# Later raw weight units, an earlier second q group, idle matmuls in the first steps and three rotating buffers in a fused retention + Mish MLP + SwiGLU kernel

## The chip, the cores and the metric

The kernel runs on one core of one Trainium2 chip. The metric is the device time of one execution in microseconds (us). Before the change, three runs took 933.38, 936.87 and 937.66 us; the median is 936.87.

## The reference

Everything is float32. q, k and v have shape [4, 8, 576, 64] (batch, head, position, head dimension); x has 2304 rows of 512.

```
scores = q @ k.T / sqrt(64)
ret    = (scores * D) @ v            D[i, j] = gamma_h ** (i - j) for i >= j, else 0
x      = ret, heads joined           [2304, 512]
h      = x @ w_in                    [512, 2048]
x      = (h * tanh(softplus(h))) @ w_out          [2048, 512]
g, val = x @ w_gate, x @ w_val       [512, 1536] each
out    = (silu(g) * val) @ w2_out    [1536, 512]
```

## The kernel before, in words

All instructions are issued in an order written out by hand; every engine works its own list in that order. A float32 product is made of three products of rounded parts (high x high, high x low, low x high), so each weight and each activation is split into a high part (a cast on ScalarE) and a low part (a subtraction on VectorE or GpSimd).

**Retention** (`retention`, from L312) has 20 steps, 5 per batch: four of 128 positions, one of 64. A step `t` (loop at L585) runs `inter` (queries times the running state, L516), `scores` (L456, L445), `state` (second half of the chunk, L497), `transposes` of the next k (L409, copied to kT by ScalarE, L411), `q_ahead` with half 1, `masks` (VectorE, L470), `products` (masked scores times v, L529, and the scaling by `gout` on VectorE, L539), the first half of the next chunk's `state`, `q_ahead` with half 0, and `scale` of v two steps ahead (GpSimd, L426). `q_ahead` (L390) says which halves of which q group (two chunks each) are transposed in which step. SyncE loads k and v four steps ahead and q six (L336 to L357). `warm` (L572) issues idle matmuls of zeros; `W` says how many.

**Raw units.** The 32 units of w_in and w_out (512 KB each) are fetched raw (`fetch`, L94, into 4 buffers), re-scaled (`rebias_raw`, L104: ScalarE L106 and VectorE L107), given sign and low bits (`sign` L111, `join` L115), and split (`part`, L117). `conversions` (L127) is the list of these pieces; retention takes one per step from step 1, and another in the steps of `EARLY` (9, 11, 14, 17), in which a first-layer product `g1` also runs.

**The Mish MLP** runs in slots `s` = 4 to 63 (`slot`, L707): `g1` (first layer, L627), then second-layer matmuls of four slots earlier (L913, L670), `mish` (ScalarE, L687), `g_hi` (L696), `g_lo` (VectorE, L700). Slots below 32 alternate between token blocks 0 and 1 (384 tokens each); slots 32 to 47 are block 2, 48 to 63 block 3. Before a block begins, its x is split (`split_hi`, ScalarE L294; `split_lo`, VectorE L299): block 2 in slots 30 and 31, block 3 in slots 44, 45 and 47.

**Background work.** Each slot from 25 (`PREP`) on ends with pieces of two lists, paced by `Pace`: a piece is issued when the sum of the paces (`RATES`) reaches its cost. `third` makes Strassen combinations of w_in for the last two token blocks (`group1`). `second` (`pieces`, L241) converts the gate and value weights: 12 groups of two raw units (`group`, L169), each loaded (`raw_load`, L149), re-scaled, joined, combined and written back to DRAM (`put`, L154, through 4 small buffers `c`); behind the first four groups stands the conversion of one unit of w2_out (`last`). Groups up to 6 ask for the next pair when their own last write is issued, into the same two buffers.

**Strassen parts.** The last two blocks' first layer runs as Strassen products (`pair1`, 8 x 7 = 56 steps, L875 te, with second-layer matmuls L913 ea between); from its second 7 steps on, each step ends with a part of `second`, and from step 45 (`AHEAD`) VectorE and ScalarE also make the operands of the next part (`ysteps`, L821, L828, L832). Then the gate and value products follow (L875 t, L1051 fa).

## Time and profile before

| | before |
|---|---|
| median of 3 runs | 936.87 us (933.38 to 937.66) |
| profiled execution: own time, span | 936.48 us, 934.7 us |
| busy: TensorE, weight load | 907.2 us (97%), 847.4 us (91%) |
| busy: VectorE, ScalarE, GpSimd | 545.5 us, 378.6 us, 50.9 us |
| mean granted TensorE clock | 0.984 |
| chain that ended last | TensorE 84%, VectorE 6%, DMA 5%, ScalarE 3%, issue 2% |

PE is TensorE's matmuls, PEld its weight loads, DVE is VectorE, ACT ScalarE, POOL GpSimd; SPq and ACTq are the queues on which SyncE and ScalarE issue transfers. Times in the trace count from the start of the span. The granted clock is a share of 2.4 GHz; 0.50 is the level of 1.2 GHz.

### The profile page before, as it was taken

To read this page: it belongs to the slowest core of one execution; us is meant where nothing else is said; L and a number is where in the kernel's file an instruction comes from. 1 tells how busy PE (TensorE), PEld (TensorE's weight loads), DVE (VectorE), ACT (ScalarE), POOL (GpSimd) and SP (SyncE) were. 2 spreads that over 40 slices of the span, in tenths; PEclk is the share of its full clock that TensorE was granted. 3 is DMA by queue.
4 is the path that set the end of the run, shared out by engine and by line. 5 is a ranking of instruction groups with operands and counts; after the bars stand their busy time and mean duration, and the time that the engine had idled before them with its cause. 6 is when DMAs were issued, how large, how long until landed. Compare 5 with 4: busy or idle time off the path is not lost.

```text
span 934.7 us, 17118 instructions
## 1 busy us (share of the span) xinstructions
PE 907.2 (97%) x6788; PEld 847.4 (91%) x6788; DVE 545.5 (58%) x1090; ACT 378.6 (41%) x788; POOL 50.9 (5%) x55
## 2 busy tenths in 40 slices
PE   7899899999999799999999999999999999999998
PEld 7788799999899799989998999999999999999997
DVE  1343468767797686567764666666544556544444
ACT  2475556644654454445444333323222223222222
POOL 2253400000000000000000000000000000000000
PEclk7799999999999899999999999999999999999999
DMA  9967445554697666599866566644745544644421
GB/s 198 226 147 176 114 117 172 155 154 154 242 294 255 214 205 225 170 305 320 300 209 240 190 204 204 206 159 154 229 161 164 159 161 154 228 161 159 158 91 68
DMA packets 125648, 177.68 MB, mean 190 GB/s; under 512 B 47104, under 2 KB 84608, under 8 KB 125568
## 3 DMA queue, kind: packets, MB, share of 16 engines
q1 hardware_dynamic: 123904, 176.19, 59.9%
q8 instruction: 54, 0.88, 0.4%
q10 hardware_dynamic: 1664, 0.39, 0.2%
q14 instruction: 26, 0.21, 0.1%
HBM read 133.04 MB, written 43.52 MB: 189 GB/s over the span
## 4 chain that ended last, share of the span: by engine, by line
PE 84%; DVE 6%; DMA 5%; ACT 3%; issue 2%; SPq 0%; POOL 0%; DVEq 0%; ACTq 0%; POOLq 0%
PE t L875 27%; PE fa L1051 16%; PE h L627 10%; PE ea L913 6%; PE da L913 6%; PE te L875 6%; PE acc L670 3%; PE o L516 2%; PE state L497 2%; PE o L529 2%; DMA rawv<-in_moe_w_val_dram 1%; DMA rawg<-in_moe_w_gate_dram 1%; PE tk L409 1%; PE tq L378 1%; PE s L456 1%
## 5 line engine op out<-in xcount | busy, mean ns | idle before, releaser
L875 PE MATMUL t<-y,su 128*128 128x384 f32 x1512 | 306.5, 338 | 1.2 <-ACT p L1123 0.7
L875 PEld LDWEIGHTS t<-y,su 128*128 128x128 f32 x1512 | 270.8, 188 | 24.8 <-DVE cv L882 1.8
L1051 PE MATMUL fa<-fu,g 128*128 128x512 f32 x648 | 190.0, 395 | 0.1
L627 PE MATMUL h<-xs,u 128*128 128x384 f32 x672 | 129.6, 339 | 7.5 <-ACT xs L294 5.0
L627 PEld LDWEIGHTS h<-xs,u 128*128 128x128 f32 x672 | 117.0, 190 | 9.9 <-ACT xs L294 5.3
L1051 PEld LDWEIGHTS fa<-fu,g 128*128 128x128 f32 x648 | 118.5, 188 | 7.6 <-ACT g L1074 0.5
L1074 ACT CAST g<-sg 128x384 fp32r<-128x384 f32 x72 | 37.0, 513 | 173.8 <-DVE sg L1110 120.5
L913 PE MATMUL ea<-ge,u 128*128 128x512 f32 (+1 forms) x384 | 75.9, 336 | 0.0
L913 PE MATMUL da<-g,u 128*128 128x512 f32 (+1 forms) x384 | 71.7, 336 | 0.0
L875 PE MATMUL te<-ye,eu 128*128 128x384 f32 x336 | 67.9, 337 | 1.0 <-DVE ve L882 1.0
L913 PEld LDWEIGHTS ea<-ge,u 128*128 128x128 f32 x384 | 62.0, 188 | 5.7
L913 PEld LDWEIGHTS da<-g,u 128*128 128x128 f32 x384 | 60.4, 188 | 6.6
L1099 ACT ACTIVATE sg<-sg 128x384 f32<-128x384 f32 x54 | 28.4, 526 | 90.7 <-DVE sg L882 90.7
L1079 DVE TENSOR_TENSOR g<-sg,g 128x384 fp32r<-128x384 f32 x72 | 40.2, 558 | 40.6 <-ACT g L1074 40.6
L670 PE MATMUL acc<-g,u 128*128 128x384 f32 x336 | 62.7, 335 | 0.0
L700 DVE TENSOR_TENSOR g<-m,g 128x384 fp32r<-128x384 f32 x60 | 33.4, 557 | 45.7 <-ACT g L696 45.7
L875 PEld LDWEIGHTS te<-ye,eu 128*128 128x128 f32 x336 | 56.8, 188 | 3.2 <-DVE ve L882 1.3
L670 PEld LDWEIGHTS acc<-g,u 128*128 128x128 f32 x336 | 58.7, 188 | 0.0
L687 ACT ACTIVATE m<-h 128x384 f32<-128x384 f32 x64 | 31.3, 489 | 44.6 <-PE h L627 44.1
L882 DVE TENSOR_TENSOR u<-t,p 128x384 f32<-128x384 f32 x36 | 20.0, 556 | 44.0 <-PE t L875 40.6
L882 DVE TENSOR_TENSOR v<-t,p 128x384 f32<-128x384 f32 x36 | 20.0, 556 | 35.3 <-PE t L875 34.6
L696 ACT CAST g<-m 128x384 fp32r<-128x384 f32 x64 | 32.9, 514 | 1.8
(129 smaller groups left out, 1055.0 us busy)
## 6 DMA issues: line engine op xcount, KB each, us to landing
su<-comb SPq DMA_DIRECT2D x126, 512.0 KB, 3.3
comb<-c SPq DMA_DIRECT2D x84, 256.0 KB, 2.6
eu<-ecomb SPq DMA_DIRECT2D x28, 512.0 KB, 5.3
raw<-in_moe_w_in_dram SPq DMA_DIRECT2D x16, 512.0 KB, 4.0
raw<-in_moe_w_out_dram SPq DMA_DIRECT2D x16, 512.0 KB, 3.7
ecomb<-e_s SPq DMA_DIRECT2D x32, 256.0 KB, 2.3
rawg<-in_moe_w_gate_dram SPq DMA_DIRECT2D x12, 512.0 KB, 5.8
ecomb<-u SPq DMA_DIRECT2D x24, 256.0 KB, 4.7
```

The lines of the kernel that those rows point to most:

```text
L627: nc.tensor.matmul(ps, lhsT=u[:, a, kk * 128:(kk + 1) * 128], rhs=s[:, e, :], start=(c == 0), stop=(c == n - 1),)
L670: nc.tensor.matmul(accs[b][d][:, :T], lhsT=u[:, a, d * 128:(d + 1) * 128], rhs=g[:, e, :], start=(i == 0 and c == 0), stop=(i == F1 - 1 an ...
L687: nc.scalar.activation(w, hs.pop(s), AF.Mish)
L696: nc.scalar.copy(out=gs[s][:, 0, :], in_=ws[s])
L700: eng.tensor_tensor(out=g[:, 1, :], in0=ws.pop(s), in1=g[:, 0, :].bitcast(F32), op=ALU.subtract)
L875: nc.tensor.matmul(p, lhsT=w[:, a, kk * 128:(kk + 1) * 128], rhs=y[kk][:, x, :], start=begin and kk == 0 and (a, x) == (0, 0), stop=kk == ...
L882: nc.vector.tensor_tensor(out=out_, in0=a, in1=b_, op=ALU.add)
L913: nc.tensor.matmul(o, lhsT=u[:, a, d * 128:(d + 1) * 128], rhs=y[:, :512] if r == 0 else y[:, 512:], start=f == 0 and (a, x) == (0, 0) and ...
L1051: nc.tensor.matmul(accs["f", b][m], lhsT=gs[u, e, h][:, x, m * 128:(m + 1) * 128], rhs=fu[2 * (u % PAIRS) + e][:, a, :], start=first, stop ...
L1074: nc.scalar.copy(out=gs[u, e, h][:, 0, :], in_=x)
L1079: nc.vector.tensor_tensor(out=g[:, 1, :], in0=x, in1=g[:, 0, :].bitcast(F32), op=ALU.subtract)
L1099: nc.scalar.activation(x, bank_ if part_ is None else x, AF.Silu)
```

## The change

- `fetch` of raw units: in retention at steps 0, 2 and 4 (before: 0, 1, 2, 4), and from the third `first` piece on instead of the second; one more fetch after the loop.
- `gout` is loaded by SyncE behind k and v of step 1, not by ScalarE; q group 1 is loaded ahead of k of step 2.
- The first half of q group 1 is transposed at the end of step 0, the second early in step 1; `masks` is issued ahead of `transposes` and `q_ahead`.
- Idle matmuls: 10 instead of 3 ahead of the first `state`; 3 at the start of steps 0 and 1, 2 ahead of their `products`. They write another bank.
- Block 2's x is split whole in slot 30, in which no background piece runs; none in slot 31.
- `second`: paces 1.9, 1.2 and 1.1 instead of 2.1, 1.3 and 1.3; the first unit of a pair is re-scaled and joined ahead of the second; each unit is loaded on its own; the buffers of groups 5 to 7 rotate over three; the empty pieces behind groups go.

```diff
--- before.py
+++ after.py
@@ -47,10 +47,10 @@
     NA = 10
     RAW, XS = 4, 6
     OFF = 2
-    W = (12, 3, 3)
+    W = (12, 3, 10, 3, 3, 2)
     PREP = 25
     NC = 4
-    RATES, AHEAD = (2.1, 1.3, 1.3, 1.15, 3.3), 45
+    RATES, AHEAD = (1.9, 1.2, 1.1, 1.15, 3.3), 45
     EARLY = (9, 11, 14, 17)
 
     xp = ctx.enter_context(tc.tile_pool(name="xp", bufs=1))
@@ -131,6 +131,7 @@
                 sign(j)
                 if j:
                     part(j - 1, splits[0])
+                if j > 1:
                     fetch()
             yield 1.4, first
             if j + 1 < len(todo):
@@ -171,13 +172,12 @@
         keys = [f"{'gv'[z]}{i}_{e}" for e in range(2)]
         v = {}
 
-        def load():
-            for e in range(2):
-                raw_load(keys[e], cols((w2_gate, w2_val)[z], 2 * i + e), False, e + 2 * (n >= FREE and n % 2))
-                lo, hi = words(keys[e])
-                for h in range(2):
-                    v[f"a{e + 1}{h + 1}"] = lo[:, h * KH:(h + 1) * KH].bitcast(F32)
-                    v["s" + "1324"[2 * e + h]] = hi[:, h * KH:(h + 1) * KH].bitcast(F32)
+        def load(e):
+            raw_load(keys[e], cols((w2_gate, w2_val)[z], 2 * i + e), False, BUFFERS.get(n, ((0, 1), (2, 3))[n % 2 == 0])[e])
+            lo, hi = words(keys[e])
+            for h in range(2):
+                v[f"a{e + 1}{h + 1}"] = lo[:, h * KH:(h + 1) * KH].bitcast(F32)
+                v["s" + "1324"[2 * e + h]] = hi[:, h * KH:(h + 1) * KH].bitcast(F32)
 
         def puts(*names):
             for nm in names:
@@ -185,9 +185,8 @@
                 put(v[nm], comb[i][c // 2][:, c % 2], f"c{i}_{c}", nc.vector)
 
         return load, [
-            (0.55, lambda: rebias_raw(keys[0])), (0.55, lambda: rebias_raw(keys[1])),
-            (0.7, lambda: sign(keys[0])), (0.7, lambda: join(keys[0])),
-            (0.7, lambda: sign(keys[1])), (0.7, lambda: join(keys[1])),
+            (0.55, lambda: rebias_raw(keys[0])), (0.7, lambda: sign(keys[0])), (0.7, lambda: join(keys[0])),
+            (0.55, lambda: rebias_raw(keys[1])), (0.7, lambda: sign(keys[1])), (0.7, lambda: join(keys[1])),
             (0.85, lambda: puts("a11", "a12")), (0.85, lambda: combine(v, ("s1", "s3"))),
             (0.45, lambda: puts("a22")), (0.85, lambda: combine(v, ("s2", "s4"))),
             (0.85, lambda: puts("s1", "s3")), (0.85, lambda: puts("s2", "s4")),
@@ -224,7 +223,11 @@
             (0.85, lambda: combine(v, ("s2", "s4"))), (0.85, lambda: puts("s2", "s4")),
         ]
 
-    FIRST, FREE = 4, 7
+    FIRST, FREE = 4, 8
+    BUFFERS = {**{n: (0, 1) for n in range(FIRST + 1)}, 5: (2, 0), 6: (1, 2)}
+    BEGIN = {4: ((5, 0),), **{n: ((n + 1, 0), (n + 1, 1)) for n in range(FREE, 2 * PAIRS - 1)}}
+    END = {**{n: ((n + 1, 0), (n + 1, 1)) for n in range(FIRST)},
+           4: ((5, 1), (6, 0)), 5: ((6, 1), (7, 0)), 6: ((7, 1), (8, 0), (8, 1))}
 
     def last(i):
         key = f"f{i}"
@@ -240,21 +243,19 @@
 
     def pieces():
         gr = [group(n) for n in range(2 * PAIRS)]
-        gap = [(0.8, lambda: None)] * 2
+        yield 0.0, lambda: gr[0][0](0)
+        yield 0.0, lambda: gr[0][0](1)
+        yield from [(0.8, lambda: None)] * 2
         for n, (load, steps_) in enumerate(gr):
-            f_load, behind = last(n) if n < FIRST else (None, gap)
-            if n == 0:
-                yield 0.0, load
-                yield from gap
-            if n >= FREE and n + 1 < len(gr):
-                yield 0.0, gr[n + 1][0]
-                behind = []
-            yield from steps_[:2]
+            f_load, behind = last(n) if n < FIRST else (None, [])
+            for m, e in BEGIN.get(n, ()):
+                yield 0.0, lambda m=m, e=e: gr[m][0](e)
+            yield from steps_[:3]
             if f_load:
                 yield 0.0, f_load
-            yield from steps_[2:]
-            if n < FREE:
-                yield 0.0, gr[n + 1][0]
+            yield from steps_[3:]
+            for m, e in END.get(n, ()):
+                yield 0.0, lambda m=m, e=e: gr[m][0](e)
             yield from behind
 
     class Pace:
@@ -390,13 +391,13 @@
             def q_ahead(t, half):
                 b, sc, n = steps[t]
                 due = (
-                    ((b, 1, 1),) if b else (),
-                    ((b, 2, 0),) if b else ((b, 1, 1), (b, 1, 0)),
+                    ((b, 1, 1),) if b else ((b, 1, 0),),
+                    ((b, 2, 0),) if b else ((), (b, 1, 1)),
                     ((b + 1, 0, 0),) if b else ((b + 1, 0, 0), (b, 2, 0)),
                     ((b + 1, 0, 1),),
                     ((b + 1, 1, 0),),
                 )[sc]
-                if half < len(due):
+                if half < len(due) and due[half]:
                     q_transposes(*due[half])
 
             def transposes(t):
@@ -552,7 +553,6 @@
             for c in range(2):
                 nc.scalar.dma_start(out=mask[C * c:C * c + C], in_=mask_d[C * c:C * c + C, C * c:C * c + C])
             nc.scalar.dma_start(out=gv, in_=gv_d)
-            nc.scalar.dma_start(out=gout[:, :, :128], in_=gout_d)
             nc.scalar.dma_start(out=gstep, in_=gstep_d)
             for e in range(2):
                 nc.scalar.dma_start(
@@ -560,18 +560,19 @@
                 )
             load(1, "k", k)
             load(1, "v", v)
+            nc.sync.dma_start(out=gout[:, :, :128], in_=gout_d)
+            load_q(2)
             load(2, "k", k)
-            load_q(2)
             load(2, "v", v)
             load(3, "k", k)
             load(3, "v", v)
 
 
-            idle = ps1.tile([128, 2, 512], F32, tag="s", name="idle")
+            idle = pha.tile([128, T], F32, tag="h", name="idle")
 
             def warm(n):
                 for _ in range(n):
-                    nc.tensor.matmul(idle[:, 0, :128], lhsT=zero, rhs=zero, start=True, stop=True)
+                    nc.tensor.matmul(idle[:, :128], lhsT=zero, rhs=zero, start=True, stop=True)
 
             warm(W[0])
             q_transposes(0, 0, 0)
@@ -583,12 +584,15 @@
             state(0, 0)
             scale(1)
             for t in range(len(steps)):
+                if t < 2:
+                    warm(W[3 + t])
                 inter(t)
                 scores(t)
                 state(t, 1)
+                masks(t)
                 transposes(t + 1)
                 q_ahead(t, 1)
-                masks(t)
+                warm(W[5] if t < 2 else 0)
                 if t in EARLY:
                     g1(EARLY.index(t))
                     zeroth.one()
@@ -613,9 +617,10 @@
                     load_q(4)
                     load_q(5)
                 load_q(t + 6)
-                if t in (0, 1, 2, 4):
+                if t in (0, 2, 4):
                     fetch()
             splits[0] = nc.vector
+            fetch()
 
     with tc.manual_schedule():
         def prod(ps, u, nm, j):
@@ -712,10 +717,8 @@
             if not i and s >= 2 * F1:
                 g1(s)
             d, nm = xt, "x"
-            if s < 2 * F1 - 2:
-                parts = ()
-            elif s < 2 * F1:
-                parts = [(2, 2 * (s % 2) + k) for k in range(2)]
+            if s < 2 * F1:
+                parts = [(2, kk) for kk in range(KT)] if s == 2 * F1 - 2 else ()
             elif b + 1 == NC:
                 parts = ()
             else:
@@ -730,7 +733,7 @@
             if s >= 2 * F1 + LAG:
                 g2_out(s - LAG)
             zeroth(RATES[4])
-            if s >= PREP:
+            if s >= PREP and not (parts and s < 2 * F1):
                 third(RATES[3])
                 second(RATES[s >= NS - F1 + 3])
 
```

## Rows read from the trace of the kernel before

**Rows 1.** The page, busy time of each engine

```profile
PE 907.2 (97%) x6788; PEld 847.4 (91%) x6788; DVE 545.5 (58%) x1090; ACT 378.6 (41%) x788; POOL 50.9 (5%) x55
```

**Rows 2.** A 23.4 us stretch: busy per engine, granted clock, DMA share, GB/s

```profile
304.20:327.60 23.40, 17.18 (x88) 16.46 (x87) 15.13 (x35) 11.51 (x27) 1.19 (x2) 0.85 0.62 217
```

**Rows 3.** TensorE's waits over the span: us in total, times, longest

```profile
PE h L627 <- ACT xs L294: 5.0, 1, 5.0
PE o L529 <- DVE p L470: 2.8, 2, 2.2
PE h L627 <- DVE xs L299: 2.5, 2, 1.3
...
PE s L445 <- issue: 1.8, 1, 1.8
...
PE te L875 <- DVE ve L882: 1.0, 1, 1.0
PE o L516 <- DVE qT L380: 1.0, 1, 1.0
PE t L875 <- ACT p L1123: 0.7, 1, 0.7
```

**Rows 4.** SyncE's waits over the span

```profile
SPq L102 <- POOL u L122: 39.3, 7, 10.9
```

**Rows 5.** Timeline of TensorE in the first five steps

```profile
10.64 0.85 PE L497 MATMUL state<-vs,k 64*64 64x64 f32 x16 [2.29 <-POOL vs L426]
...
32.88 0.69 PE L529 MATMUL o<-p,vs 64*64 64x64 f32 x32
...
45.22 0.62 PE L516 MATMUL o<-qT,sbd 64*64 64x64 f32 x13
```

**Rows 6.** Two stretches of retention, columns as in rows 2

```profile
11.00:22.00 11.00, 10.54 (x216) 9.74 (x212) 1.45 (x3) 2.28 (x6) 5.13 (x5) 0.53 1.02 210
...
41.00:45.20 4.20, 4.18 (x50) 3.38 (x49) 1.45 (x3) 0.96 (x2) 1.70 (x2) 0.59 0.77 252
```

**Rows 7.** Timeline: three idle matmuls (two instructions each)

```profile
7.52 0.83 PE L574 MATMUL idle<-zero 128*128 128x128 f32 x6
```

**Rows 8.** Raw unit 0: its issue by SyncE, and that transfer's time to landing

```profile
19.42 2.19 SPq L102 DMA_DIRECT2D raw<-in_moe_w_in_dram  x1
...
DMA to landing us min/median/max: 6.5/6.5/6.5
```

**Rows 9.** Timeline: issue of gout on ScalarE's queue

```profile
3.15 0.60 ACTq L555 DMA_DIRECT2D gout<-const_dram  x1
```

**Rows 10.** The page, transfers by line: KB each, median us to landing

```profile
raw<-in_moe_w_in_dram SPq DMA_DIRECT2D x16, 512.0 KB, 4.0
```

**Rows 11.** Timeline at block 2's split

```profile
228.36 0.48 ACT L687 ACTIVATE m<-h 128x384 f32<-128x384 f32 x1
...
238.17 3.23 PE L627 MATMUL h<-xs,u 128*128 128x384 f32 x17 [1.32 <-DVE xs L299]
```

**Rows 12.** Timeline before block 3: a load, its second half's first piece

```profile
301.89 1.33 SPq L151 DMA_DIRECT2D rawg<-in_moe_w_gate_dram  x2
...
308.54 0.68 ACT L106 ACTIVATE rawg<-rawg 128x512 f32<-128x512 f32 x1 [0.74 <-DMA rawg<-in_moe_w_gate_dram]
```

**Rows 13.** Timeline of VectorE: the four kinds of background pieces

```profile
240.20 0.76 DVE L107 TENSOR_SCALAR rawv<-rawv 128x512 uint32<-128x512 uint32 x2
240.87 0.69 DVE L111 SCALAR_TENSOR_TENSOR rawv<-rawv 128x512 uint32<-128x512 uint32 x1
...
242.41 0.88 DVE L167 TENSOR_TENSOR e<-e 128x256 f32<-128x256 f32 x2
...
475.20 0.76 DVE L157 TENSOR_TENSOR c<-rawv,c 128x256 fp32r<-128x256 f32 x2
```

**Rows 14.** Strassen part one, its end; columns as in rows 2

```profile
479.00:497.00 18.00, 18.00 (x106) 16.84 (x105) 13.15 (x27) 8.05 (x18) 0.00 (x0) 1.00 0.49 166
```

**Rows 15.** Transfers by queue, 38 to 39 us: packets, MB, engine share

```profile
q1 hardware_dynamic: 750, 0.19, 114.5%
q8 instruction: 1, 0.02, 8.8%
```

## The prediction

> **What bounds the kernel now.** I read the page first: TensorE is busy for 907.2 of 934.7 us [rows 1]. So what can be won is 27 us of idle time and whatever runs at the low clock; work taken from another engine is worth only what TensorE waits for it. The table of stretches then shows that it lies in retention, and in one stretch in which TensorE was busy for 17.2 of 23.4 us at a granted clock of 0.85 [rows 2]. TensorE's waits name the causes [rows 3]: 5.0 us for the split of a token block on ScalarE and 2.5 us for its second half on VectorE (two waits, 1.3 and 1.2); 2.8 us for masked scores; 1.8 us of "issue"; 1.0 each for q transposes and for one Strassen sum. SyncE's own waits show one more thing: 39.3 us of standing behind a raw unit whose buffer GpSimd had not emptied, with the k, v and q loads queued behind it [rows 4]. That one costs TensorE nothing by itself in rows 3.
>
> The early steps are the other loss. The first state product starts at 10.6, after 2.3 us without work; step 2's last products start at 32.9, step 5 at 45.2 [rows 5]. From 11 to 22 TensorE was busy for 10.5 of 11 us, but the mean granted clock was 0.53; at 41 to 45, after the 1.8 us gap, it was 0.59 [rows 6]. So a gap of about 2 us before a stretch brings the 1.2 GHz level, and the loss of the second drop is 4.2 x (1 - 0.59) = 1.7 us.
>
> **Retention, part by part.** Three parts act together. (a) Idle matmuls: 7 more before the first state product, 10 more in steps 0 and 1. Three cost 0.83 us at the high level [rows 7], 0.28 each. The seven lie in the 2.3 us wait for v and cost nothing (7 x 0.28 = 2.0); the ten cost 2.8 us at most, and if the clock stays low up to twice that. (b) masks moved ahead of the transposes' copies, and q group 1 transposed in step 0 and early in step 1: this removes the 2.2 us of rows 3 (the longest of the 2.8) that masked scores waited behind a q copy, and the 1.0 for the q copy itself. (c) Loads: raw units 1 to 3 leave the start.
>
> What would be late next? From step 2's products to step 5 are 12.3 us, three steps of 4.1 [rows 5]. Were the high level held from 10.6, two and a half such steps and 2.8 us of idle matmuls would bring step 2's products near 24. But the piece that rescales raw unit 0 still stands at the end of step 1, on ScalarE and VectorE, and raw unit 0 is asked for at 19.4 and lands 6.5 us later, at 25.9 [rows 8]. Today the piece comes late enough not to wait. Sooner, it waits, and step 2's masks stand behind it on VectorE, the state copy and k copy on ScalarE. So step 2's products start at 25.9 + 0.4 (shift) + 0.7 (mask) = 27.0, against 32.9: 5.8 us sooner. Before them TensorE idles for some 3 us, and I charge one clock drop of 1.6 (3.2 us at the low level, as after the gap of rows 6). From there to step 5 I leave the 12.3 us of today (45.2 - 32.9), with its "issue" wait, since the transfers around it are the same. Term: 5.8 - 1.6 = **4.2 us**. Bounds: 2.4 us worse (low level throughout: the ten idle matmuls at twice 0.28, 5.6, for the 3.2 that (b) removes) and 9 us better (no drop, and the 1.8 with its 1.7 gone).
>
> The constant gout goes from ScalarE's queue, where its issue took 0.60 us, to SyncE's, ahead of q group 1, k2 and raw unit 0 [rows 9]; bytes and engines stay. I take nothing for it: it also frees v's first transfer from a competitor. The Trainium skill ("DMA: Bandwidth & Descriptors", Issuing engines are not separate DMA queues) says that transfers of all issuing engines interleave on the same 16 engines and that the choice saves only issue time. By that rule the move wins no bandwidth and puts 0.6 us ahead of raw unit 0: the term would be 3.6 and the total 0.6 higher. No run here shows it yet.
>
> Raw units 3 to 8 are then asked for one program piece before their first use instead of several. Their landing took 4.0 us in the median [rows 10]. I take nothing: SyncE no longer meets a buffer still in use there, so it reaches the request up to a step early. After retention the wait on the same buffer decides, and nothing moves.
>
> **Block 2's split** in one go at slot 30. Now ScalarE reaches that slot's activation at 228.4, and TensorE, wanting the last quarter at 236.9, waits until 238.2 [rows 11]. The activation, four casts, g's cast and its subtraction and four subtractions, estimated at 0.5 each, end by 228.4 + 11 x 0.5 = 233.9, and no piece of the background work runs in that slot. Term: **1.3 us**, bounds 0 and 1.3.
>
> **Block 3's split.** The chain of waits runs through the background conversion of the gate and value weights: the load of a new pair is issued at 301.9 only after the old pair is written out, its second half starts on ScalarE at 308.5 [rows 12], and the split queued behind it is 5.0 + 1.2 = 6.2 us late. Stretch 304 to 328 also lost 0.15 x 23.4 / 2 = 1.75 us to the clock [rows 2]. With the change, the paces give at slot 46: before 22 slots x 2.1 = 46.2 units, after 21 x 1.9 = 39.9, so 6.3 units less are behind it. A group of 8.6 units costs VectorE 7 subtractions at 0.38, 4 combinations at 0.44, 2 shifts at 0.38 and 4 sign or join steps at 0.69 [rows 13]: 7.9 us, 0.92 per unit. That is 5.8 us, and the load itself moves from slot 45 to slot 48, behind the split. Both together exceed 6.2 us. Full gain 7.9; I take **7.0**, since slot 46 now holds four writes whose small buffers can wait for their transfers. Bounds 3 and 7.9.
>
> **The Strassen wait of 1.0** [rows 3] came of a pair asked for two steps before use. Now half of it is loaded a group earlier and the other half three steps ahead. Term **1.0**, bounds 0 and 1.1. Removing the empty pieces costs nothing: TensorE's work covers them.
>
> **What the slower pace pushes back.** By the paces, the background work ends some ten steps later, in step 52 of the 56 of the first Strassen part, not 43. In steps 45 to 55 VectorE also makes the next part's operands: it was busy for 13.2 of 18.0 us there [rows 14]. One group and two subtractions more, 8.7 us, make 21.9: 3.9 us of backlog. Two products lie between a sum and the next use of its bank, which hides some of a backlog; at the part's end, where TensorE already waited 0.7 [rows 3], nothing does. I charge half: **2.0 us lost**, bounds 0 and 4.
>
> **Sum.** 4.2 + 1.3 + 7.0 + 1.0 - 2.0 = 11.5 us against the profiled execution's own 936.5 (span 934.7 and 1.8 around it). It lies 0.4 below the median of the runs, 936.9. I predict **925 us**. A measurement of this kernel can tell about 0.5%, 4.7 us, from no change.
>
> **Rivals.** (1) *The idle matmuls don't hold the clock* (chance 0.15): they only add work at the low level, and retention gives -2.4 instead of 4.2: 936.5 - (1.3 + 7 + 1 - 2 - 2.4) = 931.6. For it: 10.5 us of busy TensorE left the clock at 0.53 [rows 6]. Against: there a gap of 2.3 us had come just before [rows 5], which the seven now fill. (2) *Block 3's wait only moves* (0.10): another write or load stands ahead of slot 47's split, only 3 of its 7.9 us are won, and the backlog costs 4: 936.5 - (4.2 + 1.3 + 3 + 1 - 4) = 931. (3) *Fetches go free* (0.12): the "issue" wait at 41 follows a packet of the instruction queue at 38 to 39, among 750 packets of data [rows 15]: I take it for a fetch that came late. Fewer raw units in the start could remove it and its drop, 3.5 us, and block 3's and the backlog's terms come at their better ends: 936.5 - (7.7 + 1.3 + 7.9 + 1 - 0) = 919. The Trainium skill ("Runtime: NRT & Kernel Launch", Instruction fetch mechanics) holds the fetch to be mostly hidden; by it that wait has another cause, and the sum stays at 925. No row here separates the two. (4) *Slower* (0.05): the raw units 3 to 7, asked for one piece ahead in steps 8 to 17, stop ScalarE and VectorE as raw unit 0 does. If each lands only after 6.5 us [rows 8] and SyncE comes to it only in its own step of some 4 us, every one waits 2.5 and drops the clock once: 5 x (2.5 + 1.6) = 20.5, and 925 + 20.5 = 945.5. It decides where request to landing exceeds the distance to the next piece; at 4.0 [rows 10] it doesn't. (5) *The split is not sooner in effect*, because VectorE reaches slot 30 late: 1.3 us, within the range.
>
> **Numbers.** The forecast, with terms within a few us of mine, has 0.58. The range reaches from the better bounds of most terms (914) to rival 2 with a poor start (934); beyond it lie rival 4 and the ends of the rest, some 0.2. Faster by over 0.5% (below 932.2) is the forecast (0.56 of its 0.58), rival 3, and half of rivals 1 and 2: 0.80; within 0.5%: the rest, 0.15; slower: 0.05.
>
> **What would show it.** Right: no wait of TensorE for xs L299 near 237 or xs L294 near 305, and a clock of 1.00 in 304 to 328; step 2's products near 27 with VectorE or ScalarE waiting for raw unit 0; a clock above 0.9 from 11 to 22; some waits on te or t between 485 and 510. Wrong: a clock near 0.5 from 11 to 22, a new wait for a raw unit in steps 9 to 17, or a split still late at block 3.

## The result, and the profile after

Four runs of the changed kernel took 920.96, 921.2, 922.67 and 922.98 us, median 921.93; four of the kernel before on the same chip 933.38 to 937.66, median 936.35. The ratio is 0.9851 (95% interval 0.9823 to 0.9878): faster by 14 us, 1.5%, where 11.5 had been forecast. The profiled execution took 920.96 us, span 919.1, mean granted clock 0.994 (0.984 before).

The page's busy times and its row of the granted clock, which answer to [rows 1]:

```profile
PE 903.7 (98%) x6822; PEld 844.2 (92%) x6822; DVE 546.5 (59%) x1090; ACT 376.9 (41%) x788; POOL 50.6 (6%) x55
...
PEclk9799999999999999999999999999999999999999
```

TensorE's idle time fell from 27.5 to 15.4 us (span less busy), and only the second of the 40 slices, 23 to 46 us, still shows a low clock. TensorE's waits over the span, against [rows 3] (us in total, times, longest):

```profile
PE s L457 <- issue: 2.5, 2, 1.6
PE o L530 <- DVE p L471: 2.1, 1, 2.1
PE t L878 <- DVE scratch L885: 1.3, 2, 0.7
...
PE t L878 <- ACT p L1126: 1.0, 1, 1.0
PE state L498 <- issue: 0.9, 2, 0.6
```

The waits for xs (5.0 and 2.5) and the one for te (1.0) are gone; "issue" is now the largest, and t has waits at the end of Strassen part one. To see where the time came from, I compare the start of the same instruction in both timelines, one where each stage begins:

| first ... | before | after | won in the stage before it | forecast |
|---|---|---|---|---|
| products of step 2 | 32.9 | 27.0 | 5.9 | 5.8 |
| inter of step 5 | 45.2 | 40.7 | -1.4 | -1.6 |
| da (retention done) | 119.0 | 110.7 | 3.8 | 0 |
| acc behind block 2's split | 253.8 | 243.9 | 1.6 | 1.3 |
| te (Strassen part one) | 376.8 | 359.6 | 7.2 | 7.0 |
| fa (gate and value products) | 524.7 | 509.2 | -1.6 | -1.0 (1.0 less 2.0) |
| end | 934.7 | 919.1 | 0.1 | 0 |

Stretches of after (columns as in [rows 2]): the one of [rows 2], that of [rows 6] from 11 to 22, and four of 2 us at steps 2 to 4.

```profile
304.20:327.60 23.40, 22.73 (x130) 22.24 (x130) 18.78 (x43) 12.23 (x30) 1.21 (x2) 1.00 0.62 217
...
11.00:22.00 11.00, 10.42 (x287) 9.47 (x287) 4.28 (x8) 3.61 (x8) 5.44 (x6) 1.00 0.95 191
26.00:28.00 2.00, 0.79 (x34) 0.66 (x34) 1.15 (x3) 1.65 (x4) 0.00 (x0) 0.98 1.28 233
28.00:30.00 2.00, 1.87 (x18) 1.65 (x18) 1.17 (x3) 0.37 (x1) 0.00 (x0) 0.50 1.19 265
36.00:38.00 2.00, 2.00 (x29) 1.67 (x30) 0.78 (x3) 1.29 (x3) 0.00 (x0) 0.50 1.31 173
38.00:40.00 2.00, 1.97 (x48) 1.69 (x44) 0.59 (x2) 1.58 (x3) 0.93 (x1) 0.96 1.25 219
```

TensorE is busy for 22.7 of 23.4 us where it was busy for 17.2, at 1.00. The clock stands at 1.00 from 11 to 22 (0.53 before). In retention it falls once, behind a gap of 2.1 us, and stays at 0.50 from 28 to 38. What made that gap, in the timeline of after (start, us, instruction, in brackets the idle time before it and its releaser):

```profile
20.59 0.58 SPq L102 DMA_DIRECT2D raw<-in_moe_w_in_dram  x1
...
25.94 0.43 DVE L107 TENSOR_SCALAR raw<-raw 128x512 uint32<-128x512 uint32 x1 [4.10 <-DMA raw<-in_moe_w_in_dram]
25.94 0.70 ACT L106 ACTIVATE raw<-raw 128x512 f32<-128x512 f32 x1 [3.65 <-DMA raw<-in_moe_w_in_dram]
26.28 0.68 DVE L471 TENSOR_TENSOR p<-s,mask 128x512 f32<-128x512 f32 x1
...
27.02 0.69 PE L530 MATMUL o<-p,vs 64*64 64x64 f32 x32 [2.08 <-DVE p L471]
```

This is the predicted chain: raw unit 0 lands at 25.94, VectorE and ScalarE have stood for it for some 4 us, and behind it come mask and products, at 27.0.

One thing had not been foreseen: steps 5 to 19 won 3.8 us. TensorE's larger "issue" waits of after in the timeline, and the hardware queues in the microseconds that hold the instruction-queue packet ahead of each (44 to 45 and 50 to 51; packets, MB, share of the 16 engines):

```profile
46.83 0.46 PE L457 MATMUL s<-qT,kT 64*64 64x64 f32 x15 [0.93 <-issue]
52.62 0.58 PE L457 MATMUL s<-qT,kT 64*64 64x64 f32 x24 [1.61 <-issue]
```

```profile
q1 hardware_dynamic: 691, 0.19, 123.9%
q8 instruction: 1, 0.02, 8.6%
...
q1 hardware_dynamic: 937, 0.25, 108.9%
q8 instruction: 1, 0.02, 5.6%
```

Before, there were such waits at 41.0 (1.79), 82.5 (1.44) and 104.8 (1.46), some 3 us behind packets at 38 to 39, 79 to 80 and 102 to 103, with data shares of 114.5% [rows 15], 109.2% and 125.4%. The last two are rows of the waits of before that [rows 3] leaves out:

```profile
PE o L516 <- issue: 1.5, 1, 1.5
PE o L529 <- issue: 1.4, 1, 1.4
```

After has none later than 52.6, though twelve more packets come in retention, in microseconds with data shares of 0 to 101.4%.

### The profile page after: what moved, and what is told of

Its sections match the earlier page's. It is cut to its first block, busy times and chain, and to the rows that moved or that the text cites. A ratio compares the mean times of both kernels' runs of the same rounds, so it can differ in the third digit from the quotient of the medians.

```text
span 919.1 us, 17207 instructions
## 1 busy us (share of the span) xinstructions
PE 903.7 (98%) x6822; PEld 844.2 (92%) x6822; DVE 546.5 (59%) x1090; ACT 376.9 (41%) x788; POOL 50.6 (6%) x55
## 4 chain that ended last, share of the span: by engine, by line
PE 87%; DVE 4%; issue 2%; DMA 2%; ACT 2%; SPq 2%; POOL 1%; DVEq 0%; POOLq 0%; ACTq 0%
PE t L878 28%; PE fa L1054 16%; PE h L632 13%; PE da L916 7%; PE acc L675 6%; PE ea L916 6%; PE te L878 5%; PE o L517 1%; PE state L498 1%; PE o L530 1%; SPq L358 1%; PE acc L891 1%; DVE y L835 1%; PE tq L379 1%; PE tk L410 1%
## 5 line engine op out<-in xcount | busy, mean ns | idle before, releaser
L632 PE MATMUL h<-xs,u 128*128 128x384 f32 x672 | 127.2, 336 | 0.0
L632 PEld LDWEIGHTS h<-xs,u 128*128 128x128 f32 x672 | 115.6, 188 | 1.4
L885 DVE TENSOR_TENSOR u<-t,p 128x384 f32<-128x384 f32 x36 | 20.0, 556 | 44.0 <-PE t L878 40.7
L701 ACT CAST g<-m 128x384 fp32r<-128x384 f32 x64 | 32.9, 514 | 1.8
```

Source lines behind the costliest of these rows:

```text
L632: nc.tensor.matmul(ps, lhsT=u[:, a, kk * 128:(kk + 1) * 128], rhs=s[:, e, :], start=(c == 0), stop=(c == n - 1),)
L701: nc.scalar.copy(out=gs[s][:, 0, :], in_=ws[s])
L885: nc.vector.tensor_tensor(out=out_, in0=a, in1=b_, op=ALU.add)
```

## The experiments

The theory after the result: the idle matmuls hold the clock; raw unit 0's landing sets step 2; at block 3 the slower pace, with the loads moved, takes the background work out of the split's way; and steps 5 to 19 went faster because the moved raw units leave DMA room for TensorE's instruction blocks. The rivals: the idle matmuls do nothing; the loads, or the pace, alone free block 3; the raw units' place is worth nothing. Each kernel is the changed one with one edit; "first da" (110.7 in after) tells the end of retention. "before" stands for the kernel before on the same chip.

| run | median us (runs) | ratio to before, 95% | first da |
|---|---|---|---|
| after | 921.93 (4) | 0.9851, 0.9823 to 0.9878 | 110.7 |
| e1 | 926.55 (4) | 0.9922, 0.9892 to 0.9953 | 113.1 |
| e2 | 920.29 (4) | 0.9848, 0.9821 to 0.9875 | 108.6 |
| e3 | 921.4 (4) | 0.9856, 0.9828 to 0.9884 | 113.4 |
| e4 | 929.68 (10) | 0.9955, 0.9936 to 0.9974 | 109.7 |
| e5 | 920.98 (4) | 0.9855, 0.9831 to 0.9879 | 110.2 |
| e6 | 920.4 (4) | 0.9848, 0.9816 to 0.988 | 111.2 |
| e8 | 920.26 (4) | 0.9854, 0.9819 to 0.9889 | 110.3 |
| e9 | 921.33 (4) | 0.9864, 0.9832 to 0.9896 | 113.1 |
| e13 | 919.21 (5) | 0.9839, 0.9812 to 0.9867 | 110.7 |
| e10, e11, e12 (one run each) | 937.56, 925.78, 921.79 | | 117.8, 115.8, 110.3 |

Retention is the same code in after, e3, e4 and e6. Its end lies between 109.7 and 113.4 there, and the masks of step 5 start between 38.4 (e4) and 41.9 (after); a difference of under 4 us in such a time decides nothing by itself.

**e1: without the new idle matmuls.**

```diff
-    W = (12, 3, 10, 3, 3, 2)
+    W = (12, 3, 3, 0, 0, 0)
```

> The changed kernel with the idle matmuls as before the change: 3 ahead of the first state product, none in steps 0 to 2; everything else kept. Theory A (the idle matmuls hold TensorE's clock): the granted clock falls to 0.5 within steps 0 and 1, step 2's last products start 1 to 4 us after the 27.0 of the changed kernel, and the whole takes 925 to 928 us. Theory B (the earlier masks and q transposes do it alone): steps 0 and 1 run at 1.00 without them, or the wait for raw unit 0 (landed at 25.9) hides the difference: products at 27.0 again and 921 to 923 us.

It lost 4.6 us between the medians. The stretch from 11 to 22 and the wait for step 2's masks:

```profile
11.00:22.00 11.00, 10.51 (x248) 9.24 (x244) 3.53 (x6) 3.89 (x8) 5.17 (x6) 0.69 0.88 182
```

```profile
28.35 0.96 PE L530 MATMUL o<-p,vs 64*64 64x64 f32 x32 [2.79 <-DVE p L471]
```

With the same real work TensorE's clock is 0.69, not 1.00. So the idle matmuls do hold it, and the total is 4.6 us shorter with them (the two intervals do not overlap). The seven ahead of the first state product and the ten behind it were not tried apart, and where the 4.6 us arise is not shown. The profiled execution of e1 is its fastest (923.56, 2.6 above that of after). Its step 2 is 1.3 us later than in after, but the masks of step 5 start at 40.0, sooner than the 41.9 of after, and the 2.4 us at first da are within the spread.

**e2: raw units asked for as before.**

```diff
-                if j > 1:
+                if j:
...
-                if t in (0, 2, 4):
+                if t in (0, 1, 2, 4):
...
-            fetch()
```

> The changed kernel with the raw units asked for as before the change (steps 0, 1, 2, 4, and from the second first-piece on). Theory A (the later requests give the 3.8 us that steps 5 to 19 won beyond the forecast, by freeing the k, v and q loads behind them): step 5 starts 0 to 1.5 us later than 40.7, and from step 5 to the first second-layer matmul it takes 73 to 75 us again instead of 70.1; 925 to 928 us. Theory B (that gain has nothing to do with the raw units; it is where the issue waits happen to fall): 70 to 71.5 us for that part, and 921 to 924 us.

The late issue waits did not come back (the longest was 1.2 us, at 46) and retention ended at 108.6. Step 2's masks start later (28.1, not 26.3), since raw unit 0 lands at 27.7, but those of step 5 at 41.0. The part of the change that comes first in its description, later raw units, wins nothing that can be seen in the total, and it is not what made steps 5 to 19 faster: that part of the theory fell.

**e3 and e4: block 3's split.** e3 takes back the paces. e4 takes back the order and the buffers of the loads, but not the empty pieces that stood behind the groups before.

```diff
-    RATES, AHEAD = (1.9, 1.2, 1.1, 1.15, 3.3), 45
+    RATES, AHEAD = (2.1, 1.3, 1.3, 1.15, 3.3), 45
```

> The changed kernel with the paces 2.1, 1.3 and 1.3 of before; the rotation of buffers, the split of block 2 and all else kept. Theory A (block 3's split was late because too much background work stood ahead of it): TensorE waits again 3 to 7 us for xs before slot 48 and the clock drops there; the backlog at the end of the first Strassen part goes, winning 2.5 back; 923 to 928 us. Theory B (it was the load asked for too late, and the new buffers alone heal it): no wait there, and 918 to 920 us, better than the changed kernel.

```diff
...
-    FIRST, FREE = 4, 8
...
+    FIRST, FREE = 4, 7
+    BUFFERS = {n: (0, 1) for n in range(FREE)}
+    BEGIN = {**{n: ((n + 1, 0), (n + 1, 1)) for n in range(FREE, 2 * PAIRS - 1)}}
+    END = {**{n: ((n + 1, 0), (n + 1, 1)) for n in range(FREE)}}
```

> The changed kernel, its slower paces and the first unit re-scaled ahead of the second kept, but a pair's two loads again both asked for when the last group's final write is issued (up to group 6), into the same two buffers. With the paces of before and the new loads TensorE waited only 0.7 us for xs at block 3. Theory A (the loads were the cause, asked for too late): a wait of 1 to 6 us before slot 48 returns, and one of about 1 us near the seventh pair; 923 to 929 us. Theory B (either half is enough, since pace or load alone moves the pair's load behind slot 47): no wait above 1 us there; 921 to 923 us.

From first acc to first te, over block 3's split, after needs 115.8 us (123.0 before), e3 115.6, e4 115.8. The wait is gone in both, but for 0.7 us in e3. This does not make pace and loads two halves of which either is enough, because e4's edit does not reach this split: the pair in question (the fifth) is asked for in the same way, into the same two buffers, in before, after, e3 and e4. What decides is on which side of slot 47's split that pair's re-scaling stands, since it waits for the load. Counted from the paces and costs in the code, it stands in slot 46 before, in slot 47 in e3 (where only slot 30, without pieces, puts it back) and in slot 49 in after and e4; within a slot, the split is issued ahead of the pieces. ScalarE before, at the split that stands behind the re-scaling of [rows 12], and ScalarE in e3, where the split comes first:

```profile
309.48 0.93 ACT L294 CAST xs<-x 128x384 fp32r<-128x384 f32 x2
```

```profile
296.23 0.92 ACT L295 CAST xs<-x 128x384 fp32r<-128x384 f32 x2
...
301.91 0.69 ACT L106 ACTIVATE rawg<-rawg 128x512 f32<-128x512 f32 x1 [1.45 <-DMA rawg<-in_moe_w_gate_dram]
```

So the theory that pace and loads were both needed fell. The slower paces win nothing in the total either (921.93 with them, 921.4 without). A run that fills slot 30 again and keeps the rest was not made.

But e4 pays later, at the begin of Strassen part one. TensorE's waits of e4, ScalarE's wait ahead of the first of them, and a step of its chain of waits ahead of the second (start, us):

```profile
PE te L877 <- DVE scratch L884: 3.1, 1, 3.1
PE te L877 <- ACT scratch L981: 3.1, 1, 3.1
```

```profile
365.06 0.68 ACT L106 ACTIVATE rawg<-rawg 128x512 f32<-128x512 f32 x1 [6.53 <-DMA rawg<-in_moe_w_gate_dram]
```

```profile
397.39 4.80 DMA rawv<-in_moe_w_val_dram
```

From first te to first t it needs 135.2 us against 126.0 in after. With two buffers, a pair is asked for when the last one's buffers come free, and in e4 its re-scaling follows at once: by the count in the code, the seventh pair is asked for in slot 63 and re-scaled in slot 63, the eighth in steps 13 and 14 of the part. Before, the empty pieces put two slots or steps between (57 and 59, 8 and 10). In after, half of each of these pairs is asked for a group earlier, into the third buffer. So with the empty pieces out, the new loads and their third buffer are what saves these 9 us. That it is the slower pace that needs them is not shown: no run has the paces of before with the loads of e4.

**e6: the third pace back to 1.3, the first two left.**

```diff
-    RATES, AHEAD = (1.9, 1.2, 1.1, 1.15, 3.3), 45
+    RATES, AHEAD = (1.9, 1.2, 1.3, 1.15, 3.3), 45
```

> The changed kernel with the pace of the background work in the first Strassen part at 1.3, as before, instead of 1.1. Theory A (VectorE's backlog at the end of that part costs the 2.7 us): the waits of t for VectorE (scratch) go, from the first te to the first fa it takes 148 us (147.9 before) instead of 149.6, and 919 to 920.5 us. Theory B (something else there, such as the table load or the write-backs): 149 to 150 us again, and 921 to 923 us.

From first te to first fa: 147.9 us, against 149.5 in after; from 480 on TensorE has one wait on t left, where after has three:

```profile
PE t L878 <- ACT p L1126: 0.7, 1, 0.7
```

The eight runs with the pace of 1.1 and the new loads, after among them, need 149.0 to 149.5 us, so the slow third pace costs 1.2 to 1.7 us: the backlog is real. The total moved by 1.5 us, less than the intervals can tell.

**e5 and e9: the wait for raw unit 0.** e5 takes the first piece in step 2 instead of step 1; e9 leaves it and puts eight idle matmuls into the gap.

```diff
-                if t:
+                if t > 1:
                     zeroth.one()
```

> The changed kernel with the list of raw-unit pieces begun in step 2 instead of step 1, so that the rescaling of raw unit 0 is not queued ahead of step 2's masks. Theory A (that wait and the clock drop behind it are the largest loss left in retention): no wait for raw unit 0, step 2's products start near 24 instead of 27.0, the clock stays at 1.00 from 11 to 45, step 5 starts 5 to 8 us before 40.7; 914 to 917 us. Theory B (the next transfer is late instead: q5, landing near 25, or k and v): step 5 starts at most 3 us earlier, with a clock drop in steps 2 to 4; 919 to 921 us.

```diff
-                warm(W[5] if t < 2 else 0)
+                warm(W[5] if t < 2 else 8 if t == 2 else 0)
```

> The changed kernel with 8 more idle matmuls in step 2, in the 2.1 us in which TensorE waits for the masks behind raw unit 0. They cost at most 0.3 us where they overrun. Theory A (that gap brings the low clock from 27.9 to 38): the clock stays at 1.00, step 5's masks come 3 to 5 us before 41.9, and the end of retention 2 to 5 us before 110.7; 917 to 920 us. Theory B (the clock falls whatever fills the gap, or the instruction fetches become late in the steps that run faster): step 5's masks at most 1.5 us sooner, with an issue wait of 1 to 2.5 us in steps 3 to 6; 920.5 to 923 us.

In e5 the wait is gone, and the masks of step 2 start 2.4 us sooner (23.9, not 26.3). Then TensorE waits for issue twice, the second time behind a packet of the instruction queue at 30 to 31:

```profile
26.87 0.67 PE L498 MATMUL state<-vs,k 64*64 64x64 f32 x14 [0.90 <-issue]
33.66 0.49 PE L530 MATMUL o<-p,vs 64*64 64x64 f32 x7 [2.55 <-issue]
```

```profile
q1 hardware_dynamic: 998, 0.27, 129.0%
q8 instruction: 1, 0.02, 8.0%
```

The clock falls all the same, and the masks of step 5 start at 41.8, as in after (41.9). In e9, with the gap filled, the clock does not fall: its mean over the whole span is 1.000, in each of the four runs. The masks of step 5 start at 39.9, and three issue waits follow:

```profile
45.33 0.69 PE L457 MATMUL s<-qT,kT 64*64 64x64 f32 x31 [1.71 <-issue]
...
55.42 0.71 PE L517 MATMUL o<-qT,sbd 64*64 64x64 f32 x14 [1.44 <-issue]
60.65 0.56 PE L446 MATMUL s<-qT,kT 64*64 64x64 f32 x11 [1.04 <-issue]
```

Both had first da at 110 or later, and the total is that of after. That the issue waits took back what was won is argued: 39.9 and 41.8 lie within the 38.4 to 41.9 of the same code.

**e8: gout back on ScalarE's queue.**

```diff
+            nc.scalar.dma_start(out=gout[:, :, :128], in_=gout_d)
...
-            nc.sync.dma_start(out=gout[:, :, :128], in_=gout_d)
```

> The changed kernel with gout loaded by ScalarE's queue as before. If the issuing queue saves only issue time (the page's rule): raw unit 0 lands 0.3 to 0.8 us before the 25.9 of the changed kernel and step 2's products start that much before 27.0; the total the same within 1 us. If the transfer itself competes with the first v: the first state product starts up to 1 us later, and raw unit 0 lands at 25.9 or later. By neither does the total move by more than 1 us.

Raw unit 0 was asked for sooner (19.2, not 20.6) and landed later (26.7, not 25.9), and step 0's masks start at 13.8, not 12.5. Neither can be put down to gout: where the code up to there is that of after (e3, e4, e6, e9), raw unit 0 lands anywhere from 25.5 to 26.6 and step 0's masks start from 12.5 to 13.7. The total is the same.

**e10 to e12: what the issue waits come from.** e10 is the kernel before once more; e11 adds one load of 512 KB, into a tile that nobody reads, in each of steps 8 to 17; e12 makes four idle matmuls of 384 columns out of the first twelve of 128, so that each later step stands at an earlier place in TensorE's list of instructions.

```diff
+                if 8 <= t < 18:
+                    extra = cp.tile([128, H, 2, D], F32, tag="extra", name=f"extra{t}", bufs=2)
+                    nc.sync.dma_start(out=extra, in_=q[t % B, :, :256, :].rearrange("h (p r) d -> p h r d", r=2))
```

```diff
-            zero = cp.tile([128, 128], F32, tag="zero", name="zero")
+            zero = cp.tile([128, T], F32, tag="zero", name="zero")
...
-            warm(W[0])
+            warm(W[0] // 3, T)
```

> The kernel of before, unchanged, profiled once more, to see how far its retention differs between executions. Four profiles of kernels with the changed retention ended it between 109.7 and 113.4. Theory A (the 6.4 us won in steps 8 to 19 are two issue waits and a clock drop that fall by chance): steps 8 to 19, from mask to mask, take 50 to 54 us here instead of 56.2, with fewer or shorter issue waits. Theory B (the order of the old kernel makes them each time): 55 to 57 us and issue waits of 1.4 us or more again near 81 and 103.

> The changed kernel with one more load of 512 KB of q in each of the steps 8 to 17, into a tile that nothing reads; it changes no result. Theory A (the issue waits are instruction blocks of TensorE that come late behind data): steps 8 to 19 take 53 to 60 us instead of 49.8, with two or more issue waits of 0.5 to 2.5 us, each within 4 us after a packet of the instruction queue in a microsecond of full data queues. Theory B (the waits have another cause, and k and v come early enough): 50 to 51.5 us and no issue wait above 0.5 us there.

> The changed kernel with the first 12 idle matmuls of 128 columns replaced by 4 of 384: the same columns, 16 or 32 fewer instructions of TensorE, so every later instruction block begins at another place of the program. If issue waits are late blocks, those of the changed kernel (0.9 at 46, 1.6 at 51, none later) change in place and length: other steps, 0 to 2.5 us each, retention ending anywhere from 109 to 114. If they belong to certain steps of the program, they stay in steps 6 and 7 with 0.9 and 1.6 within 0.4.

e10 has issue waits again in the late steps (1.17 at 79.6, 1.04 at 84.8, 1.73 at 101.8) besides 1.36 at 17.5 and 1.50 at 45.4, and block 3's wait of 6.0. From the masks of step 8 to those of step 19 it needs 57.5 us, of which 4.6 are issue waits (before 56.2, 3.5 of them issue). e11 needs 57.4, 4.7 of them issue, with the DMA engines at 0.96 of their time there (0.64 in after). The eleven runs of the changed kernel and its variants without extra loads need 49.8 (after) to 53.1, with 0 to 2.9 us of issue waits. Two of e11's issue waits, and the queues at 69 to 70 and 80 to 81:

```profile
72.36 0.79 PE L635 MATMUL h<-xs,u 128*128 128x384 f32 x3 [2.04 <-issue]
82.97 0.34 PE L457 MATMUL s<-qT,kT 64*64 64x64 f32 x8 [1.62 <-issue]
```

```profile
q1 hardware_dynamic: 794, 0.22, 124.1%
q8 instruction: 1, 0.02, 7.6%
...
q1 hardware_dynamic: 646, 0.28, 116.4%
q8 instruction: 1, 0.02, 7.6%
```

In e12 the waits end at 44.1, 53.4, 75.9 and 80.5, where after has 46.8 and 52.6 and none later. That alone says little, since the same code has late ones too in other executions (1.04 at 79.0 in e3, 0.93 at 76.9 in e6). The longest of e12, 2 to 3 us behind an instruction packet at 73, and that of e3:

```profile
75.88 0.49 PE L410 MATMUL tk<-ident,k 128*128 128x128 f32 x3 [2.25 <-issue]
```

```profile
79.04 0.68 PE L498 MATMUL state<-vs,k 64*64 64x64 f32 x15 [1.04 <-issue]
```

What settles it is how many matmuls TensorE had behind it at each wait (the number behind the x of the first bracket; columns as in [rows 2], from 0 to just ahead of the wait's end). After at 46.8, e12 at 44.1, e3 at 79.0, e12 at 75.9:

```profile
0.00:46.50 46.50, 41.71 (x855) 37.57 (x856) 14.43 (x27) 19.94 (x39) 14.97 (x19) 0.89 1.02 213
```

```profile
0.00:43.80 43.80, 39.44 (x855) 33.55 (x856) 15.06 (x28) 20.34 (x39) 15.74 (x20) 0.96 0.98 217
```

```profile
0.00:78.80 78.80, 71.76 (x1615) 64.56 (x1616) 27.55 (x53) 38.40 (x76) 31.50 (x35) 0.91 0.94 209
```

```profile
0.00:75.50 75.50, 68.01 (x1615) 59.06 (x1616) 27.95 (x53) 38.79 (x77) 31.50 (x35) 0.98 1.01 221
```

Over the two kernels and the twelve runs, 34 issue waits of 0.9 us or more lie in retention. Every one stands behind 222, 476, 602, 729, 855, 982, 1108, 1235, 1362, 1489, 1615, 1742 or 2122 matmuls, within one. These numbers lie 126.7 or a multiple of it apart, and the weight loads come as often. It is the count that decides and not the step: behind 855, scores wait in after, the state product in e12 and the transposes of k in e1. The queue q8 brings one packet for each such place; the page of after has 6822 matmuls, 53.9 times 126.7, and its row of q8 is

```profile
q8 instruction: 54, 0.88, 0.4%
```

So these waits belong to the boundaries of blocks in TensorE's list of instructions, and q8's packets are these blocks. Whether a block is late is in the packet records of the traces, which give each packet's start and length (1.4 us for that of 44 to 45 in after, which ends at 45.4; the wait behind it ends at 46.8). All 34 waits end 1.25 to 1.81 us behind the end of the packet for their place, and at none of the 252 such places in the 14 retentions does TensorE go on sooner than 1.2 us behind it. In after, TensorE takes some 5 us from one place to the next in retention, and some 22 us behind it; there, in no run, a packet ends less than 7 us before TensorE goes on at its place.

Which places have a wait changes from one execution to the next. At 156 of the 252 places, data took 73% of the engines or more in the 2 us around the packet's start. There the packet started 2.3 us (median) after TensorE had passed the place before, and 31 of the waits follow; at the other 96 it was 1.1 us, with three waits. With e11 this says that more data traffic makes blocks late. Why before and e10 lose more to them in steps 8 to 19 than the changed kernel stays open: not the raw units' order (e2), not gout (e8), and hardly the total of the traffic there (share 0.69 before, 0.64 after). q's and the masks' new order were not tried alone.

**e13: e2 and e6 together**, the two edits that had each come out 1.5 us lower than after, if within the error.

> The changed kernel with the raw units asked for as before (the second run, 920.3) and the pace of 1.3 in the first Strassen part (920.4). If both gains are real and add, 917.5 to 919.5 us and from the first te to the first fa 147.8; if the first was only where the issue waits fell in that run, 919.5 to 921 us.

Five runs gave 917.0 to 920.23, median 919.21: 2.7 us below after and the lowest of all. From first te to first fa it needs 148.2 us; first da at 110.7 is that of after. Its ratio's interval overlaps that of after, so the 0.3% is no proof of a faster kernel.

## Why the prediction was right, and where its sum was not

The forecast 925 was 3 us too high, and 921.9 lies inside the range. By its steps:

- **Step 2's products at 27.0**: so it came, by the chain foretold (raw unit 0 at 25.94, mask at 26.28). The 5.9 us won are those against one execution of before; in e10, before once more, these products start at 30.2. That VectorE and ScalarE work in order, so that a piece moved sooner hands its wait for data to the masks behind it, was the step that mattered.
- **From there to step 5**: 1.6 us for one clock drop, then the 12.3 of before, 13.9 in all. The 13.7 that came (27.0 to 40.7) agree by luck, by two errors that cancel in this execution. The low level lasted 10 us, 28 to 38, not the 3.2 read from [rows 6] (whose 1.7 lost would be 3.4): at half speed 5 us, 3.4 more than charged. And the 1.8 us issue wait of before with its own clock drop of 1.7, left in, did not come: 3.5 less. In e4, the same code, the low level ends at 32 and the masks of step 5 start 3.5 us sooner than in after. Rival 3 had the second part right, but its reason was fewer raw units in the start, and e2, with the old requests, does not have the wait at 41 either.
- **Steps 5 to 19, a term put at nothing**: the prediction had nothing for them and they won 3.8 us, nearly all of the 4.0 by which the profiled execution beat the forecast. It gave a reason for taking nothing for the raw units there; that the other waits would stay it took without one. One pair of executions gives 8.3 us for all of retention, against 4.2; but the same code varies by 3.7 us in its end. By the means of the two executions of before (119.0, 117.8) and the four of after's code (110.7, 113.4, 109.7, 111.2) the term is 7.1, between 4.4 and 9.2. By the same means, 4.5 of it are won by step 5's masks (44.5 and 40.0) and 2.6 behind them. Before loses 1.4 us and more at a time there to issue waits (2.9 in the two at 82 and 105; 3.9 in the three late ones of e10). The prediction had read one issue wait, in the early steps, and never searched the late ones.
- **Raw units 3 to 8 later, nothing; gout, nothing**: right (e2, e8). The Trainium skill ("DMA: Bandwidth & Descriptors", Issuing engines are not separate DMA queues) holds that the issuing engine saves only issue time. For the total the runs agree (920.26 and 921.93). The consequence that the prediction drew from it, raw unit 0 later by 0.6, is not seen: the unit landed at 25.5 to 26.6 with the move and at 26.7 without it (e8), and differences of this size come between executions of the same code.
- **Block 2, 1.3**: 1.6. **Block 3, 7.0**: 7.2, and the clock there rose to 1.00 as foretold. But the sum behind it, 5.8 us less work on VectorE and the moved load to exceed 6.2, was too strict. In e3 only one slot's pieces, 2.1 of the 6.3 units, are gone ahead of the split, and all but 0.7 of the wait goes with them. The wait came of the pair's re-scaling, which stands ahead of the split until its load lands; putting it behind the split is enough, as the prediction's own move of the load from slot 45 to slot 48 does.
- **Strassen wait 1.0**: gone. **Backlog -2.0**: the stage lost 1.6 with that 1.0 won in it, so the backlog cost 2.6. It shows in the three waits on t at the part's end (2.3 us, 0.7 before), and e6 puts 1.2 to 1.7 of it down to the third pace alone.
- **Rival 1** (idle matmuls hold nothing) fell: 1.00 with them, 0.69 without (e1). **Rival 2** fell: block 3's wait went and did not move. **Rival 4** fell: TensorE has no wait for a raw unit in steps 8 to 17. **Rival 5** fell: the split was sooner.

## What to carry to other kernels

A piece moved sooner on an in-order engine takes the wait for its data with it: before moving it, look when its data lands and what stands behind it. At block 3 it worked the other way: one piece that waits for a load, moved behind the split, was enough. Where transfers fill the DMA engines, read the "issue" rows of all steps beside the packets of the instruction queue, and count the matmuls ahead of each wait. Short matmuls make it worse: they bring the next block's place within 5 us here. Removing the first wait (e5) or bridging it (e9) gave no time in the total here, with issue waits behind it. Empty pieces between a load and its first use can be time that the load needs: take them out only if the load is asked for earlier, as by one more buffer, or the wait comes back in the next stage (e4). Before reading a difference of a few us in one stage, see how far the same code differs there between executions; in this retention it was 3.7 us.

## What the hardware showed that was not expected

- A gap of some 2 us of TensorE is not always followed by the 1.2 GHz level, nor always for as long. In after a gap of 2.1 us was followed by 10 us at that level (28 to 38). In e4 the gap in the same step was 2.0 us, and from 32 on the clock was full again. In e3, a wait of 2.27 us that ended at 45.8 was followed by the low level through the whole stretch shown; in e12, one of 2.25 us that ended at 75.9 was not followed by it at all. So what the prediction read from two gaps [rows 6] is no rule. e4, e3 and e12:

```profile
32.00:38.00 6.00, 5.89 (x156) 5.02 (x158) 3.05 (x7) 4.70 (x10) 3.15 (x4) 1.00 1.03 216
```

```profile
46.00:52.00 6.00, 6.00 (x109) 5.32 (x106) 1.78 (x4) 2.41 (x6) 1.42 (x2) 0.50 0.83 203
```

```profile
76.00:82.00 6.00, 5.35 (x172) 4.61 (x172) 2.05 (x4) 4.41 (x9) 1.52 (x2) 1.00 0.59 157
```

- TensorE waits 0.9 to 2.6 us for issue at a time, at places 126.7 matmuls (or a multiple) apart, and goes on 1.25 to 1.81 us behind the end of a packet of the instruction queue. The Trainium skill ("Runtime: NRT & Kernel Launch", Instruction fetch mechanics) holds crossing a block boundary to be mostly hidden. The traces agree as far as most of these places go: 34 of the 252 in retention have such a wait, and from 110 us on after has none. But in this retention, with short matmuls and full queues, those that are not hidden cost before 4.7 us.
